# The second pass of a first batch: one order of GpSimd's work for another

## The chip, the cores and the metric

The kernel runs on one core of a Trainium2 chip. The metric is the device time of one execution in microseconds, as a median over runs of the same program. One further execution was recorded by the hardware profiler; all views of the profile are of that one.

## The reference

Two blocks follow one another. The first is an attention in which only scores close to the row's largest count; the second is a gated feed-forward layer.

```python
# q, k, v: (8, 8, 576, 64) float32; tau = 0.02
scores = scale * q @ k^T                       # scale = 1 / 8
thresh = max(scores, -1) - tau
scores = where(scores >= thresh, scores, -1e9)
attn   = exp(scores - max(scores, -1))
attn   = attn / (sum(attn, -1) + 1e-9)
x      = (attn @ v) as (4608, 512)             # heads side by side
g      = x @ w_gate                            # (512, 1536), float64 in memory
val    = x @ w_val                             # (512, 1536), float64
out    = (g * sigmoid(g) * val) @ w_out        # (1536, 512), float64
```

## The kernel before, in words

The kernel works through 8 batches of 4 pairs of heads. The first batch is special: while its attention runs, the weights come in and are turned from float64 into float32 by hand. It goes over its four pairs twice. The first pass (n = 0 to 3 in the loop over `segs[:2 * NP]`, NP = 4) does the tiles t = 0 and 1 of 128 queries of each pair; the second pass (n = 4 to 7, from about 57 to 134 us) does the tiles 2, 3 and 4, so a segment n has three steps x = 0, 1, 2. Tile 4 is half as long and holds both heads in one tile. Everything in this loop is issued in the order in which it is written, on each engine; from batch 1 on, a planner (`Plan`) with estimated durations orders the work. The planner starts after the loop and does not see its real times.

A step of the second pass makes the scores of a tile (TensorE, L465 or L471), the row maxima (VectorE, L484), the exponentials (ScalarE, L487), the mask and sums (VectorE, L492), the reciprocal `ri` of the sums (L495), and then scales p: head 0 on ScalarE (L502), head 1 on GpSimd (L500; steps 0 and 1 only, tile 4 has no second half). TensorE transposes p (L536) and, a step later, multiplies it by v (L569). Between these it fills in the first products of the feed-forward layer: four groups of `gate` (L585, "pg") and `value` ("pv"), spread over the pass by `fill`, so that one value product is finished in each segment. ScalarE copies the gate's product in two ways (L600, L601), VectorE combines them with the value's product (L609) into `hall`, and `gates` lets GpSimd multiply that by the gate (L616).

The weights go through these steps, one piece of 128 x 768 numbers at a time; 21 of 24 pieces are finished in the loop:

- `fetch_weights`: SP issues the loads into one of several places (L306, L309).
- `split_weights`: ScalarE makes a scaled upper part (L325, into the weight's place `dst`) and the lower words (L326, into `lo`, one of three places used in turn, `los`).
- `clamp_split`: GpSimd clamps the upper part (L318).
- `shift_weights`: VectorE shifts it by 3 bits (L345).
- `join_weights`: VectorE joins it with the sign (L351) and frees the place of the load; then, in the version before, GpSimd adds the lower words of one piece.
- `add_lower(n)`: GpSimd adds the lower words of n more pieces that are joined (L361). A piece that has been joined but not added is in `unsummed`.

A piece is split in one step, shifted in the next and joined in the one after. In the second pass a segment handles four pieces: at the end of step 2 of segments 4 to 6 ("double") two pieces are shifted and one more is split, so step 0 of the next segment joins two pieces, steps 1 and 2 one each. In segment 4 the scaling of the next batch's q (L398) follows step 1. The version before ends each step with `gates`, and each step begins with `join_weights`, so that GpSimd's order in a segment is: add, scale, clamp, add; add, scale, clamp; add, clamp, clamp, gate product.

After the loop what is left of the products is filled in, one more piece is joined and added, and `gates` is called once more; then the planner takes over with the last three pieces (L909 to L923) and batch 1.

Of the kernel before, what the change touches and what calls it, by code (L numbers as in the profile page):

```python
# [128 lines left out]
def kernel(  # L129
# [14 lines left out]
    NP = H // 2  # L144
# [117 lines left out]
    def give_back(ps):  # L262
        turns.append(taken.pop(id(ps))[0])

    def run_idle(n):
        ps = bank("idle")
        for _ in range(n):
            nc.tensor.matmul(ps[:, 0:TC], ones[:, 0:P], ones, start=True, stop=True)
        give_back(ps)
# [42 lines left out]
    def words(place, dst, w):  # L312
        return places[place].bitcast(U32).rearrange("p (m n w) -> p m n w", m=dst.shape[1], w=2)[:, :, :, w]

    early_slots, clamped, unclamped, shifted, unsummed = [True], [], deque(), [], []
# [16 lines left out]
    def clamp_split():  # L332
        while unclamped:
            dst = unclamped.popleft()
            clamp(nc.gpsimd, dst)
            clamped.append(dst)
# [8 lines left out]
            nc.vector.tensor_scalar(out=ub, in0=ub, scalar1=3, scalar2=None, op0=ALU.logical_shift_left)  # L345
        shifted.extend(steps)

    def join_weights():
        for up, place, lo in shifted:
            ub = up.bitcast(U32)  # L350
            nc.vector.scalar_tensor_tensor(out=ub, in0=words(place, up, 1), scalar=0x80000000, in1=ub,  # L351
                                           op0=ALU.bitwise_and, op1=ALU.bitwise_xor)
            used.discard(place)
        unsummed.extend(shifted)
        shifted.clear()
        add_lower(min(1, len(unsummed)))

    def add_lower(n):
        for up, place, lo in unsummed[:n]:
            ub = up.bitcast(U32)  # L360
            nc.gpsimd.tensor_tensor(out=ub, in0=ub, in1=lo.bitcast(U32), op=ALU.add)  # L361
            joined.append(up)
        del unsummed[:n]
# [155 lines left out]
    def flip_steps():  # L519
        if not unflipped:  # L520
            return
        seg, t, both, ps = unflipped.popleft()
        n = P if t < NT else D
        pT = pTbufs[0][:, 0:2 * KT * n].rearrange("p (h t q) -> p h t q", h=2, t=KT)
        pT2 = pTbufs[0][:, 2 * KT * n:(2 * KT + 1) * n]
        pTbufs.rotate(1)
        end = None
        for h, (p, unit) in enumerate(ps):
            tp = bank("tp")
            if h == len(ps) - 1:  # L530
                end = bank("end")
            for kt in range(KT):
                at_ = kt * P + (D if turned(t) and h == 1 else 0)
                ks, to = slice(at_, at_ + P), slice(kt * P, (kt + 1) * P)
                if unit is ident:
                    nc.tensor.transpose(tp[:, to], p[:, ks], unit)  # L536
                else:
                    nc.tensor.matmul(tp[:, to], p[:, ks], unit, start=True, stop=True)
            if t < NT:
                if h == 1 and not turned(t):  # L540
                    for hs, (p_, unit_) in zip(heads, ps):
                        nc.tensor.matmul(end[hs, 0:P], p_[:, KM:S], unit_, start=True, stop=True)
                elif h == 1:
                    nc.tensor.transpose(end[:, 0:P], both, unit)
                nc.scalar.copy(pT[:, h], tp.rearrange("p (t q) -> p t q", q=P))
            else:
                for hs in heads:
                    nc.tensor.matmul(end[hs, 0:D], p[hs, KM:S], unit[hs, hs], start=True, stop=True)
                nc.scalar.copy(pT, tp.rearrange("p (t h q) -> p h t q", h=2, q=D))
            give_back(tp)  # L550
            yield
        nc.scalar.copy(pT2, end[:, 0:n])
        give_back(end)
        unattended.append((seg, t, pT, pT2))

    def attend_tile(copy=lambda xa, fn: (fn(), give_back(xa))):
        if not unattended:
            return
        if not xts:
            for u, lo in enumerate((0, 2 * XW)):  # L560
                xts["full", u] = xall[:, lo:lo + XW].rearrange("p (c n) -> p c n", c=NCC)
            xts["last", 0] = xlast
        seg, t, pT, pT2 = unattended.popleft()
        vr, vr2 = seg["v"]
        n = pT2.shape[1]
        xa = bank("xa")
        for kt in range(KT):
            for h in range(2):
                nc.tensor.matmul(xa[h * D:(h + 1) * D, 0:n], vr[:, h, kt, :], pT[:, h, kt, :],  # L569
                                 start=(kt == 0), stop=False)  # L570
        nc.tensor.matmul(xa[:, 0:n], vr2, pT2, start=False, stop=True)
        u, lo = divmod(t * P, TC)
        to = xts[("last", 0) if t == NT else ("full", u)][:, seg["i"], lo:lo + n]
        copy(xa, lambda: nc.scalar.copy(to, xa[:, 0:n]))
# [39 lines left out]
    def gates():  # L614
        for ht, gt in ungated:
            nc.gpsimd.tensor_tensor(out=ht, in0=ht, in1=gt, op=ALU.mult)  # L616
        ungated.clear()
# [36 lines left out]
    def fill(n):  # L654
        credit[0] += n
        done = 0
        while credit[0] > 0:
            c = next(pieces)
            left[0] -= c
            done += c  # L660
            credit[0] = credit[0] - c if c else 0
            if not c:
                break
        return done
# [8 lines left out]
    def pace(n, x):  # L673

        return left[0] / (sum(len(seg["tiles"]) for seg in segs[n:2 * NP]) - x)
# [32 lines left out]
    def give(unit):  # L708
        ready.append(unit)
        left[0] += cost(unit)  # L710
# [19 lines left out]
    for n, seg in enumerate(segs[:2 * NP]):  # L730
        early_slots[0] = n < NP
        if n >= NP:
            seg["v"] = segs[seg["i"]]["v"]
        for x, t in enumerate(seg["tiles"]):
            go = scores(seg, t)
            next(go)
            if (n, x) != (NP - 2, 1):
                join_weights()
            if not n and not x:
                run_idle(6)  # L740
            next(last, None)
            box = []
            if n < NP:
                attend_tile(lambda *y: box.extend(y))
            else:
                attend_tile()
            flips = flip_steps()
            if n >= NP and x == 1:
                next(flips, None)
            next(go)  # L750
            if box:
                box[1]()
                give_back(box[0])
            next(last, None)
            for _ in flips:
                pass
            if n == NP and x == 0:
                attend_tile()
                give(FIRST)
            part = pace(n, x) / 2  # L760
            more = len(split)
            if n or x:
                split_weights()
                fetch_weights(2)
            next(go)
            if (n, x) == (NP - 2, 1):
                join_weights()
            if (n, x) == (NP - 2, 0):
                prepare(segs[n + 1])
            clamp_split()  # L770
            add_lower(1)
            double = t == NT and NP <= n < NP + 3
            if more and not double:
                shift_weights()
            fill(part)
            next(go)
            fill(part)
            if double:
                shift_weights(2)
                split_weights()  # L780
                clamp_split()
                fetch_weights(2)
            gates()
            last = go
            if n == NP - 1 and x == 0:
                later.rotate(1)
            if later and (n == NP or n == NP - 1 and x == 0):
                to, fr = later.popleft()
                nc.vector.transpose(out=to, in_=fr)
            if x == 0 and 0 < n < NP - 1:  # L790
                load_v(segs[n + 1])
                more_loads.popleft()()
            if n == 0 and x == 1 or n == 1:
                scales.popleft()()
            elif n == NP - 2 and x == 1:
                more_loads.popleft()()
                scales.popleft()()
            elif n == NP - 1:
                scales.popleft()()
                fetch_qk(NP)  # L800
            elif n == NP and x == 1:
                scales.popleft()()
            if x == len(seg["tiles"]) - 2 and n + 1 < len(segs) and (n, x) != (NP - 2, 0):
                prepare(segs[n + 1])
# [1391 lines left out]
```

## Time and profile before

| What | Value |
|---|---|
| runs | 1370.12 us median of three (1370.07, 1370.12, 1372.92) |
| profiled execution | 1367.33 us, its span 1365.5 us |
| granted TensorE clock | 0.999 of full speed |
| busy: TensorE, VectorE, ScalarE, GpSimd | 99%, 79%, 63%, 52% of the span |
| TensorE busy, 56.9 to 79.8 us | 21.75 of 22.9 |
| TensorE busy, 79.8 to 99.4 us | 18.58 of 19.6 |
| TensorE busy, 99.4 to 119.0 us | 18.13 of 19.6 |
| GpSimd busy in the same three stretches | 16.62, 16.74, 16.70 |

Each line of the page's groups and of a timeline gives the line of the code, the engine, the operation, the tile written and the tile read, and a duration. A timeline adds the start, and in square brackets the idle time of the engine ahead of the instruction with what ended it. A row of the stretches gives the stretch, its length, the busy time of TensorE, of its weight loads, of VectorE, ScalarE and GpSimd with the number of instructions, the granted clock, the share of the DMA engines and GB/s. In the chain that ended last, each row is a start, a time and what the program's end depended on in that time.

### The profile page before, as it was taken

Reading aid. Unit: us, or ns where it says so; the run is one execution under the profiler, and the core shown is the slowest. Engines: PE = TensorE matmul, PEld = TensorE weight load, DVE = VectorE, ACT = ScalarE, POOL = GpSimd, SP = SyncE. Lnnn points to the kernel's source line nnn. Section 1 sums busy time; section 2 is a strip of 40 time slices with the busy share of each in tenths; the row PEclk is TensorE's granted clock in tenths of the full one; section 3 lists DMA queues with packets and bytes.
Section 4 is the critical chain, followed back from the end, with each engine's and each line's share of the span. In section 5 each row is a group of like instructions: output and inputs, shape, how many; then the busy total and the mean of one; then the engine's idle time right before and its main releaser. Section 6 shows DMA issues by size and latency. Waiting matters only on the chain.

```text
span 1365.5 us, 39125 instructions
## 1 busy us (share of the span) xinstructions
PE 1347.5 (99%) x15590; PEld 1124.9 (82%) x15590; DVE 1076.7 (79%) x2860; ACT 866.7 (63%) x2222; POOL 715.7 (52%) x664
## 2 busy tenths in 40 slices
PE   8999999999999999999999999999999999999998
PEld 6777787777788788878888788888887788999888
DVE  7878998888787877787878877887788766797786
ACT  6888765677765777677767676677767673330330
POOL 2788698754655669434963387337943592000000
PEclk9999999999999999999999999999999999999999
DMA  8752424556425441654155514542255404424411
GB/s 175 202 186 88 85 49 125 142 164 179 111 52 162 146 90 36 193 144 113 38 170 135 161 19 144 149 145 66 78 155 146 109 27 160 149 75 143 159 54 32
DMA packets 208293, 162.31 MB, mean 119 GB/s; under 512 B 166128, under 2 KB 180464, under 8 KB 202736
## 3 DMA queue, kind: packets, MB, share of 16 engines
q1 hardware_dynamic: 203920, 158.86, 40.9%
q8 instruction: 123, 2.02, 0.6%
q10 hardware_dynamic: 4192, 0.95, 0.3%
q14 instruction: 58, 0.48, 0.1%
HBM read 138.28 MB, written 21.50 MB: 117 GB/s over the span
## 4 chain that ended last, share of the span: by engine, by line
PE 90%; DVE 3%; POOL 2%; DMA 2%; ACT 1%; issue 1%; SPq 1%; ACTq 0%; DVEq 0%; POOLq 0%
PE pb L1031 17%; PE pa L1031 12%; PE px L1520 12%; PE sc L1780 10%; PE pe L1031 9%; PE xa L1917 9%; PE po L1313 5%; PE py L1529 5%; PE pg L1244 2%; PE pv L1244 2%; PE sc L1198 1%; PE pe L1198 1%; PE sc L1031 1%; PE sc L465 1%; POOL pall L500 1%
## 5 line engine op out<-in xcount | busy, mean ns | idle before, releaser
L1861 DVE SCALAR_TENSOR_TENSOR pall<-sc,th,pall 128x288 f32<-128x288 f32 x504 | 244.2, 513 | 49.1 <-ACT pall L1859 32.5
L1859 ACT ACTIVATE pall<-sc,lows 128x288 f32<-128x288 f32 x504 | 233.8, 500 | 72.9 <-DVE pall L1861 38.0
L1031 PE MATMUL pb<-xall,big 128*128 128x256 f32 x1104 | 262.0, 380 | 0.0
L1031 PEld LDWEIGHTS pb<-xall,big 128*128 128x128 f32 x1104 | 207.5, 190 | 29.6 <-issue 1.6
L1896 DVE STREAM_TRANSPOSE pall<-pall 128x576 f32<-128x576 f32 x252 | 188.0, 763 | 27.7 <-POOL pall L1891 14.3
L1894 ACT ACTIVATE pall<-pall,ri 128x288 f32<-128x288 f32 x416 | 190.6, 526 | 23.4 <-DVE ri L1882 22.5
L1031 PE MATMUL pa<-xall,big 128*128 128x256 f32 x752 | 178.9, 381 | 0.3 <-ACT sc L1038 0.3
L1031 PEld LDWEIGHTS pa<-xall,big 128*128 128x128 f32 x752 | 140.7, 190 | 20.9 <-issue 2.5
L882 POOL TENSOR_TENSOR hall<-hall,tmp 128x512 f32<-128x512 f32 x80 | 102.5, 1281 | 103.1 <-DVE hall L1090 60.3
L1780 PE MATMUL sc<-kT,qT 64*32 64x288 f32 (+1 forms) x5376 | 145.7, 345 | 0.1
L1818 DVE TENSOR_REDUCE mx<-sc 128x2 f32<-128x576 f32 x168 | 118.4, 746 | 34.7 <-PE sc L1780 34.1
L1891 POOL TENSOR_SCALAR pall<-pall,ri 128x288 f32<-128x288 f32 x88 | 87.8, 1006 | 103.9 <-DVE ri L1882 74.7
L1780 PEld LDWEIGHTS sc<-kT,qT 64*32 64x32 f32 x5376 | 98.2, 106 | 50.2 <-issue 11.2
L1031 PE MATMUL pe<-xall,big 128*128 128x256 f32 x576 | 138.4, 383 | 0.5 <-ACT pall L1894 0.5
L1917 PE MATMUL xa<-pall,vall 64*32 64x288 f32 x4032 | 129.4, 404 | 3.0 <-PE px L1520 2.7
L1031 PEld LDWEIGHTS pe<-xall,big 128*128 128x128 f32 x576 | 107.6, 190 | 19.3 <-issue 4.3
L1917 PEld LDWEIGHTS xa<-pall,vall 64*32 64x32 f32 x4032 | 83.4, 107 | 41.7 <-issue 5.0
L882 POOL TENSOR_TENSOR tmp<-tmp 128x512 f32<-128x512 f32 x36 | 45.9, 1274 | 85.8 <-ACT tmp L1112 85.8
L1876 ACT COPY sums<-sums 32x6 f32<-32x6 f32 x336 | 66.6, 198 | 28.3 <-DVE pall L1861 24.2
L1089 ACT ACTIVATE vall<-tmp 128x512 f32<-128x512 f32 x96 | 60.0, 628 | 35.3 <-DVE tmp L1102 28.1
L1529 PE MATMUL py<-wo,hall 128*128 128x256 f32 x336 | 74.8, 379 | 0.0
L882 POOL TENSOR_TENSOR hall<-hall 128x384 f32<-128x384 f32 (+2 forms) x67 | 67.4, 1020 | 9.0 <-PE px L1520 8.2
(273 smaller groups left out, 2492.4 us busy)
## 6 DMA issues: line engine op xcount, KB each, us to landing
big<-sums_hbm SPq DMA_DIRECT2D x42, 1024.0 KB, 5.2
big<-sums_hbm SPq DMA_DIRECT2D x48, 768.0 KB, 4.6
vall<-in_v_dram SPq DMA_DIRECT2D x112, 144.0 KB, 3.1
out_dram<-big SPq DMA_DIRECT2D x32, 256.0 KB, 3.1
qT<-in_q_dram SPq DMA_DIRECT2D x112, 72.0 KB, 4.8
kT<-in_k_dram SPq DMA_DIRECT2D x112, 72.0 KB, 3.0
wo<-in_moe_w_gate_dram SPq DMA_DIRECT2D x16, 384.0 KB, 3.9
wo<-in_moe_w_val_dram SPq DMA_DIRECT2D x16, 384.0 KB, 4.8
```

Of the source, the lines that this page charges most:

```text
L882: return lambda: nc.gpsimd.tensor_tensor(out=out, in0=a, in1=b, op=op)
L1031: nc.tensor.matmul(ps[:, i], w[:, k_, i * P:(i + 1) * P], x[:, k_, :], start=first and i == k_ == 0, stop=True, skip_group_check=True)
L1520: nc.tensor.matmul(ps, a[:, f, :], ws[n][:, f, :], start=bank_ not in begun, stop=True, skip_group_check=True)
L1529: nc.tensor.matmul(ps(), a[:, f, i * P:(i + 1) * P], operands[o][:, f, :], start=first and f == 0, stop=True, skip_group_check=True)
L1780: nc.tensor.matmul(to[g * G:(g + 1) * G], qT[hs, col:col + G], kT[hs, c * SH + lo:c * SH + hi], start=True, stop=True)
L1818: rs.append(job("DVE", 0.72 if w > 1 else 0.42, lambda h=h: nc.vector.tensor_reduce(out=mx[:, n0 + h:n1 + h + 1:max(2, n1 - n0), 0], in_=s ...
L1859: ej = job("ACT", 0.44, lambda x=x, n=n: nc.scalar.activation(ps[x], scs[x], AF.Exp, bias=nm[:, n:n + 1]), ej, rank=top, on=on[x])
L1861: masks[x] = job("DVE", 0.48, lambda x=x, n=n: nc.vector.scalar_tensor_tensor(out=ps[x], in0=scs[x], scalar=th[:, n:n + 1], in1=ps[x], op0 ...
L1891: scaled.append(job("POOL", 1.02, lambda x=x, n=n: nc.gpsimd.tensor_scalar(out=x, in0=x, scalar1=ri[:, n:n + 1], scalar2=None, op0=ALU.mul ...
L1894: scaled.append(job("ACT", 0.46, lambda x=x, n=n: nc.scalar.activation(x, x, AF.Copy, scale=ri[:, n:n + 1]), rj, rank=rank))
L1896: seg["turned"].append(job("DVE", 0.72, lambda both=both: nc.vector.transpose(out=both, in_=both), *scaled, rank=rank))
L1917: nc.tensor.matmul(holds[a].ap()[x * G:(x + 1) * G, 0:SH].rearrange("d (i q) -> d i q", q=G), vr[rs, h, j, ds], p[rs, h, :, j, :], start=( ...
```

## The change

In the second pass only, GpSimd's instructions of a step change their order. `join_weights` adds no lower words there; after the scale of p and the clamp, up to two pieces are added, and then the gate products that are waiting are multiplied, instead of at the end of the step. A value product that is finished in a step is therefore multiplied by its gate in the next one. GpSimd's order in a segment becomes: scale, clamp, add, add, gate product; scale, clamp, add; clamp, add, clamp. The first pass and everything behind the loop are as before.

```diff
-    def join_weights():
+    def join_weights(add=1):
...
-        add_lower(min(1, len(unsummed)))
+        add_lower(min(add, len(unsummed)))
...
             if (n, x) != (NP - 2, 1):
-                join_weights()
+                join_weights(n < NP)
...
             clamp_split()
-            add_lower(1)
+            add_lower(1 if n < NP else 2)
+            if n >= NP:
+                gates()
             double = t == NT and NP <= n < NP + 3
             if more and not double:
                 shift_weights()
...
                 split_weights()
                 clamp_split()
                 fetch_weights(2)
-            gates()
             last = go
```

## The prediction, made before the changed kernel was run

> **What bounds the kernel now.** I read the page first. TensorE is busy for 1347.5 us of the span of 1365.5, so a change off TensorE counts only where it makes TensorE wait.
>
> ```profile
> PE 1347.5 (99%) x15590; PEld 1124.9 (82%) x15590; DVE 1076.7 (79%) x2860; ACT 866.7 (63%) x2222; POOL 715.7 (52%) x664
> ```
>
> Next I looked up the engines by stretch. The changed pass runs from about 57 to 134 us; one of its segments (n = 6) and the stage behind it:
>
> ```profile
> 99.40:119.00 19.60, 18.13 (x140) 13.87 (x139) 16.23 (x31) 17.20 (x33) 16.70 (x12) 1.00 0.16 47
> 152.00:400.00 248.00, 247.13 (x3276) 197.62 (x3284) 209.94 (x598) 171.96 (x480) 169.98 (x166) 1.00 0.42 114
> ```
>
> In the segment TensorE idles 1.47 us of 19.6, and GpSimd (the fifth busy time, 16.70) is nearly full. Behind the pass TensorE idles 0.87 us of 248. So what the pass loses, nothing later gives back. Third, the chain that ended last, through segment 6 (start, us, what):
>
> ```profile
> 99.36 1.87 POOL pall L500
> 101.23 1.32 POOL big L318
> 102.55 2.63 POOL big L361 x2
> ...
> 106.10 2.03 POOL pall L500
> ...
> 108.17 0.66 PE tp L536 x4
> ...
> 108.94 2.17 PE pv L585 x10
> ...
> 111.14 0.69 DVE hall L609
> 111.82 0.64 DVE wo L345 x2
> ...
> 112.68 1.41 DVE lows L484 x2
> 114.09 2.83 DVE wo L351 x2
> 116.92 0.75 DVE pall L492 x2
> ```
>
> This cycle of 19.6 us bounds the pass: from step 0's scale of p (L500) over GpSimd's clamp and two adds to step 1's scale, transposes and products, then VectorE's shifts (L345), maxima, joins (L351) and masks, to the next segment's scale. Fourth, the timelines of GpSimd and VectorE, for the order and the long instructions:
>
> ```profile
> 84.73 1.83 POOL L361 TENSOR_TENSOR big<-big 128x768 uint32<-128x768 uint32 x1
> 89.33 1.83 POOL L361 TENSOR_TENSOR big<-big 128x768 uint32<-128x768 uint32 x1
> 91.20 0.83 POOL L318 TENSOR_SCALAR big<-big 128x768 f32<-128x768 f32 x1
> 94.37 1.27 POOL L616 TENSOR_TENSOR hall<-hall,tmp 128x512 f32<-128x512 f32 x1
> 96.53 2.46 POOL L361 TENSOR_TENSOR big<-big,extra 128x768 uint32<-128x768 uint32 x1 [0.89 <-DVE big L351]
> ```
>
> ```profile
> 75.80 1.96 DVE L351 SCALAR_TENSOR_TENSOR big<-wo,big 128x768 uint32<-128x768 uint32 x2
> 85.47 1.51 DVE L345 TENSOR_SCALAR big<-big 128x768 uint32<-128x768 uint32 x1
> 87.57 0.94 DVE L351 SCALAR_TENSOR_TENSOR big<-wo,big 128x768 uint32<-128x768 uint32 x1
> 92.19 1.02 DVE L345 TENSOR_SCALAR big<-big 128x768 uint32<-128x768 uint32 x2
> 94.46 2.86 DVE L351 SCALAR_TENSOR_TENSOR big<-wo,big 128x768 uint32<-128x768 uint32 x2
> ```
>
> The reader is to see that shift and join shut out GpSimd's add and gate product, and the other way round. A shift takes 0.51 (1.02 for two); the one of 85.47 took 1.51 because the add of 84.73 ran until 86.56. Two joins take 1.96; those of 94.46 took 2.86 because the gate product ran until 95.64. The add of 96.53 took 2.46 for 1.83 because the second join ran until 97.3. An engine that waits gets in when the other's instruction ends, ahead of that one's next.
>
> **The change part by part.** T is the start of step 0's scale, U that of step 1's.
>
> *First add moved behind the scale.* In segments 5 to 7 the start of T is not GpSimd's: the reciprocal (L495) ends at 79.63, 99.19 and 118.79, and the scale starts 0.17 after it each time (the chain names a matmul there; the constant gap says otherwise). So moving the add gives T nothing directly.
>
> *Gate product moved out of the joins.* It no longer stands at the end of step 2, where it held up the joins of segments 6 and 7 (2.86 and 2.04 + 0.95 against 1.96). Gain 0.9 us each in segments 6 and 7; none in segment 5, whose joins took 1.96 already.
>
> *Between the two scales.* Before: scale 1.87, clamp 1.3, step 0's second add and step 1's first add, 3.6; together 6.73 (79.81 to 86.54, and again 99.36 to 106.10). After: scale, clamp, two adds (both of step 0), then the waiting gate product, 1.27. A shift waits there already (T + 5.66, during the second add); it gets in ahead of the gate product with 0.44 (86.54 to 86.98). So U = T + 8.4: 1.7 us more. This is on the path: step 1's reciprocal ends at 85.56, so its scale already waits 0.8 us for GpSimd, and the transposes wait for the scale. Charged in segments 5, 6, 7; in segment 4 no gate product is pending yet and its second scale (66.06) follows its reciprocal, so nothing.
>
> *Step 2's add moved behind the clamp, step 1's behind its scale.* After U's scale (2.03) GpSimd now has clamp 0.82, add 1.82, clamp 0.82, and starts the add at U + 5.5. Before, both adds were done by 91.16 and the port was free when the two shifts came at 92.19, which is U + 5.65. Now the first shift meets an add that runs until U + 7.3: 1.7 us, on the path. Segments 5 and 6. In segment 4 the same happens by another way: before, add 70.62 to 72.45, clamp until 73.56, second shift at 73.59. After, step 1's add (1.82) goes ahead of the scaling of q (1.72), step 2's clamp ends at about 73.4, the add follows until 75.2, and the second shift, which waits for the clamp's signal, comes after it: 1.6 us. In segment 7 the two shifts at the end don't exist; its shift of step 2 (1.29) is held by an add either way.
>
> *ScalarE's splits.* The ring of lower words has three places. In step 0 of segments 5 to 7 the split now stands in the program ahead of the add that reads that place, so its wait (L326 behind the add: 1.2, 1.6, 1.6 us) goes. The add then takes the newer piece's words, which changes the lowest bits and no duration. That wait was not on the path, so I take no gain. In its place step 1's split waits for step 0's second add, until T + 6.8 (before: no wait), and ScalarE's scale of p, the copies of the gate's products and step 2's exponentials are queued behind it. It ends near T + 8.6; the transposes need it with U's scale only, which ends past T + 10.3: cover 1.7 us, cost zero. If that cover were gone, the excess would be paid in full.
>
> *Loads.* SP's fetches of weights stand where they stood, behind joins, and slide with them. That matters at the end: the last fetch (133.24) waits for the last join (132.18 to 133.16), and the next q and k loads stand behind it, so the delay is handed on. GpSimd's work at the very end has a gap of 1.66 us ahead of L923 as cover for the reordered add and gate product: zero, 0 to 1.
>
> Sum: segment 4, +1.6; segment 5, 1.7 + 1.7 = +3.4; segment 6, 1.7 + 1.7 - 0.9 = +2.5; segment 7, 1.7 - 0.9 = +0.8. Total +8.3. The profiled execution took 1367.33 us (span 1365.5 and 1.8 around it) and would take 1375.6; the three runs lie at 1370.07 to 1372.92, so on their median 1370.12 I forecast 1378.4.
>
> Two costs are unknown. (a) At the end of step 2 a clamp waits for the port with the two shifts; no row shows whether a waiting GpSimd instruction gets in between two of VectorE's. If it does, 0.82 more in each of segments 4 to 6; never less than zero, since the clamp is needed later than the shifts. I take zero, since step 2's second pieces come late from ScalarE (93.58 before). (b) Step 2's join now waits during the gate product and starts with U's scale. A scaling by a per-partition value (L398 at 42.73) took 1.78 where its like takes 1.08, under a join (41.19 to 43.55): +0.7. But U's scale at 86.54 stood 0.44 under a shift and took 2.03 for 1.87: +0.16. I take zero, the nearer row being the second, with up to 0.5 more in segments 5, 6 and 7.
>
> The Trainium skill, page "SBUF — State Buffer", section "Who interferes with whom", has VectorE and GpSimd share one port pair that whoever issues first keeps for the whole instruction, the other being fully blocked. The adds agree, but the scale of p does not: the join of 87.57 ran its usual 0.94 inside the scale of 86.54 to 88.57. By the page's rule the scale would lose a whole join of 0.87 in (b), and the sum would be about +10.9.
>
> **The rivals.**
> *VectorE first.* The margin in step 2 is 0.16 us (U + 5.65 against U + 5.5). If the shifts ask for the port just before the add starts, and both pass, the 1.6 and twice 1.7 go: +3.3, 1373.4. For it: the margin is small. Against: three segments have to fall so. If some do: +5 to +6.6.
> *Harder waits.* (a) and (b) in full: 8.3 + 3 x 0.82 + 3 x 0.5 = +12.3, 1382.4. For it: waiting engines do get in at a hand-over.
> *Not slower: the joins' gain alone.* If GpSimd's longer queue in step 0 is hidden, what is left is -0.9 in segments 6 and 7: 1368.3, within 0.2%. It decides at step 1's reciprocal, T + 5.75: the scale would have to find GpSimd free by then. Even at their shortest (clamp 0.82) the instructions ahead of it need 1.87 + 0.82 + 3.64 + 1.27 = 7.6, so it needs the gate product to be elsewhere. Against it stands that the value product of each segment ends in step 2 (L609 at 91.59), so its gate product is always pending at the next step 0.
> *The change does nothing*: the order is written out, and no planner can undo it; I give this no chance of its own.
>
> **How the numbers follow.** Forecast 0.50 (1376 to 1380); harder waits 0.20; VectorE first, in all or some segments, 0.20; the joins' gain alone 0.06; unpriced gain 0.04. A measurement can tell about 0.2%, 2.7 us. Slower: 0.50 + 0.20 + 0.13 (those of VectorE first that stay above 2.7) = 0.83. Same: 0.07 + 0.06 = 0.13. Faster: 0.04. The range goes from VectorE first less the runs' scatter, 1372, to the harder waits, 1383.
>
> **What would show it.** In the profile after: T to U 8.4 us (6.7 before), with two adds and the gate product in it; the joins of step 0 at 1.96 in each segment; step 2's first shift (or the pair) long by 1.7, over an add; the wait of L326 gone in step 0 and there in step 1; a segment near 22 us; TensorE idle some 8 us more before 145 us and the same after. I am wrong if the pair of shifts is still at 1.02, if T comes early enough to pay for the gate product, or if TensorE's idle time behind the pass shrinks.

## The result, and the profile after

The changed kernel takes 1377.32 us (median of six, 1376.99 to 1378.31) against 1370.17 for the kernel before: a ratio of 1.0052, 95% interval 1.0041 to 1.0064, or 7.15 us slower. A second set of runs of the same kernel gave 1378.59 against 1370.61, ratio 1.0065 (1.0052 to 1.0078). The forecast was +8.3 us (1378.4). The profiled executions lie 9.66 us apart (1376.99 and 1367.33).

The page's first line and two of the stretches, segment 6 with its surroundings and the 248 us behind the pass:

```profile
PE 1352.2 (98%) x15590; PEld 1130.0 (82%) x15590; DVE 1079.2 (78%) x2860; ACT 867.8 (63%) x2222; POOL 715.2 (52%) x664
```

```profile
100.00:122.00 22.00, 18.77 (x129) 14.27 (x130) 14.43 (x29) 15.69 (x29) 16.68 (x11) 0.84 0.13 42
160.00:408.00 248.00, 247.50 (x3269) 198.01 (x3272) 210.24 (x600) 172.30 (x480) 170.01 (x166) 1.00 0.41 114
```

Behind the pass TensorE idles 0.50 us of 248 (0.87 before): the loss is made in the pass and kept. But TensorE is busy 4.7 us longer than before with the same 15590 products, and the granted clock in the segment is 0.84. That is new, and the forecast does not have it. The chain through segment 6:

```profile
101.91 1.87 POOL pall L500
103.78 1.31 POOL big L318
105.09 2.63 POOL big L361 x2
...
108.61 1.60 POOL hall L616
110.21 2.41 POOL pall L500
...
112.67 1.12 PE tp L536 x4
...
114.00 4.27 PE pv L585 x10
```

The gate product (L616) stands between the two scales, as forecast. The products behind the second transposes took 4.27 us where they took 2.17. VectorE's long instructions, and GpSimd's around step 2 of segment 5:

```profile
72.48 2.16 DVE L345 TENSOR_SCALAR big<-big 128x768 uint32<-128x768 uint32 x1 [0.72 <-POOL big L318]
93.74 3.06 DVE L345 TENSOR_SCALAR big<-big 128x768 uint32<-128x768 uint32 x2
98.06 1.81 DVE L351 SCALAR_TENSOR_TENSOR big<-wo,big 128x768 uint32<-128x768 uint32 x2
118.91 1.02 DVE L345 TENSOR_SCALAR wo<-wo 128x768 uint32<-128x768 uint32 x2
```

```profile
93.46 1.82 POOL L361 TENSOR_TENSOR big<-big 128x768 uint32<-128x768 uint32 x1
95.32 1.07 POOL L318 TENSOR_SCALAR big<-big 128x768 f32<-128x768 f32 x1
108.61 1.60 POOL L616 TENSOR_TENSOR hall<-hall,tmp 128x512 f32<-128x512 f32 x1
110.19 2.42 POOL L500 TENSOR_SCALAR pall<-pall,ri 128x576 f32<-128x576 f32 x1
```

The shift of segment 4 waits for the add (2.16 for 0.56), the pair of segment 5 takes 3.06 for 1.02, and the joins are down to 1.81. In segment 6 the pair is at 1.02, unhindered. TensorE's timeline says why:

```profile
78.88 2.09 PE L465 MATMUL sc<-pall 64*128 64x288 f32 x10 [2.21 <-DVE pall L492]
112.67 1.12 PE L536 MATMUL tp<-pall 128*128 128x128 f32 x4 [1.60 <-POOL pall L500]
113.79 4.47 PE L585 MATMUL pv<-xall,big 128*128 128x256 f32 x10
136.09 3.77 PE L585 MATMUL pv<-xall,big 128*128 128x256 f32 x10
```

After idle time of 2.21 us, and of 0.97 and 1.60 and of 0.72 and 0.88 a little apart, TensorE ran at a granted clock of 0.50 for a while: at 81 to 84.5, 111 to 119 and 135 to 139 us by stretches of 1 us. Products that are late by 2 us bring the shifts past the add.

The table compares intervals, read from the timelines: S is segment 4's second scale, T and U the scales of steps 0 and 1 of a segment, J the last join of the pass. A star marks an interval in which the clock stood at 0.50 for part of the time.

| | S to T5 | T5 to U5 | U5 to T6 | T6 to U6 | U6 to T7 | T7 to U7 | U7 to J | S to J |
|---|---|---|---|---|---|---|---|---|
| before | 13.75 | 6.73 | 12.82 | 6.74 | 12.86 | 6.73 | 6.49 | 66.12 |
| after | 15.17 | 7.97* | 13.80 | 8.29 | 14.84* | 8.45 | 7.02* | 75.54 |
| after, second profile | 15.17 | 7.98* | 13.81 | 8.29 | 14.20 | 8.35* | 5.35 | 73.15 |
| gate product alone | 13.59 | 8.29 | 12.18 | 8.46 | 12.18 | 8.31 | 5.34 | 68.35 |
| the same, second profile | 13.59 | 8.28 | 14.45* | 8.28 | 13.94* | 8.30 | 5.35 | 72.19 |
| adds alone | 15.32 | 8.11* | 14.72 | 7.19* | 14.52 | 8.11* | 6.71 | 74.68 |
| no add in step 2 | 13.58 | 8.29 | 12.16 | 8.46 | 12.18 | 8.29 | 5.35 | 68.31 |

J is VectorE's end of the pass, not TensorE's. TensorE's first product of the next batch (`pg`) starts 2.90 us behind J before the change (135.08) and 3.72 or 3.73 behind it in all the other rows of the table. So the delay that TensorE carries on is 0.8 us more than S to J shows.

### The profile page after: what moved, and what is told of

It is laid out like the page before. It is cut to its first block, busy times and chain, and to the rows that moved or that the text cites. A ratio compares the mean times of both kernels' runs of the same rounds, so it can differ in the third digit from the quotient of the medians.

```text
span 1374.9 us, 39125 instructions
## 1 busy us (share of the span) xinstructions
PE 1352.2 (98%) x15590; PEld 1130.0 (82%) x15590; DVE 1079.2 (78%) x2860; ACT 867.8 (63%) x2222; POOL 715.2 (52%) x664
## 3 DMA queue, kind: packets, MB, share of 16 engines
q8 instruction: 123, 2.02, 0.6%
## 4 chain that ended last, share of the span: by engine, by line
PE 90%; DVE 2%; POOL 2%; DMA 2%; issue 1%; SPq 1%; ACT 1%; ACTq 0%; DVEq 0%; POOLq 0%
PE pb L1032 17%; PE pa L1032 12%; PE px L1521 12%; PE sc L1781 10%; PE pe L1032 9%; PE xa L1918 9%; PE po L1314 5%; PE py L1530 5%; PE pg L1245 2%; PE pv L1245 2%; PE sc L1199 1%; DMA vall<-in_v_dram 1%; PE pe L1199 1%; PE sc L1032 1%; PE pv L585 1%
```

## The experiments

Two theories stood against each other. The queue theory is that of the prediction: GpSimd's order and the port that it shares with VectorE make the loss. The clock theory says that most of it is TensorE at half clock, which the longer waits set off. Each median stands against the kernel before on the same chip (1369.73 for the first four, 1370.61 for the next four).

**The two halves of the change.** First the gate product alone:

```diff
             add_lower(1)
+            if n >= NP:
+                gates()
...
-            gates()
+            if n < NP:
+                gates()
```

> Only the gate product moves, to behind the adds of the next step; the adds stay where they were. Queue theory (GpSimd's longer queue and the port it shares with VectorE set the time): between the scales of steps 0 and 1 +1.3 to +1.7 us in segments 5, 6 and 7, the joins of segments 6 and 7 short again (-0.9 each), nothing in step 2: +2 to +3.3 us in all. Clock theory (the granted TensorE clock falling to 0.50 after idle time makes most of the loss): the idle time ahead of the second transposes grows here as in the whole change, so the clock falls and the cost is 4 us or more, with a mean granted clock below 0.998.

Median 1375.77, ratio 1.0053 (1.0037 to 1.0068), so +6.0; but the six executions scatter from 1371.83 to 1379.47. The profile is of the fastest: the clock is at 1.00 throughout and S to J is 2.23 longer, as the queue theory has it (1.6 between the scales, 0.6 to 1.2 back behind each). So the median spoke for the clock and the profile for the queue. A second profile was to show whether both are true:

> The kernel with the gate product alone moved, a second profile: the first had the clock at 1.00 throughout and lost 2.2 us between segment 4's second scale and the last join, while its executions scatter by 7.6 us. If falls of the clock make that scatter, this look shows one or more stretches at half clock in the pass or none, and the same 8.3 us between the scales in every segment without one; each stretch adds 0.6 to 1.7 us.

It took 1375.37, beside 1368.66 for the kernel before, and has two stretches at half clock in the intervals of the table (a third, from 43.6 to 47.0, lies ahead of them). The second transposes of segment 5 and the products behind them, in the first profile and then in the second:

```profile
90.44 0.66 PE L536 MATMUL tp<-pall 128*128 128x128 f32 x4 [2.62 <-POOL pall L500]
...
91.05 2.32 PE L585 MATMUL pv<-xall,big 128*128 128x256 f32 x10
```

```profile
91.50 1.12 PE L536 MATMUL tp<-pall 128*128 128x128 f32 x4 [2.61 <-POOL pall L500]
...
92.62 3.40 PE L585 MATMUL pv<-xall,big 128*128 128x256 f32 x10
```

The same idle time of 2.6 us ahead of the same products is followed by the full clock in one execution and by half of it in the other. U5 to T6 is 12.18 and 14.45, U6 to T7 12.18 and 13.94: the two stretches cost 2.3 and 1.8 us, and S to J is 6.07 longer than before instead of 2.23. Each cost more than the 0.6 to 1.7 that was expected. Why the same pause costs this once and not the other time is told in the last section.

Then the adds alone:

```diff
-                join_weights()
+                join_weights(n < NP)
...
-            add_lower(1)
+            add_lower(1 if n < NP else 2)
```

> Only the adds move, behind scale and clamp; the gate product stays at the end of a step. Queue theory: the two scales stay 6.7 us apart; step 2's shifts wait for an add (+1.6 in segment 4, +1.7 each in segments 5 and 6), and the joins of segments 6 and 7 come after the gate product (-0.9 each): +3 us in all, with rows of L345 near 3 us. Clock theory: no more idle time ahead of the second transposes than before, the clock stays at 1.00, and the cost is 0 to +1.6.

Median 1378.78, ratio 1.0071 (1.0055 to 1.0087): +9.0, more than the whole change. Both expectations are missed. The clock falls in segments 5, 6 and 7, at about the start of their first scales. Apart from that the queue costs more than was thought:

```profile
97.01 2.70 DVE L345 TENSOR_SCALAR big<-big 128x768 uint32<-128x768 uint32 x2
...
100.96 2.35 DVE L351 SCALAR_TENSOR_TENSOR big<-wo,big 128x768 uint32<-128x768 uint32 x2
```

The pair of shifts waits for the add and the joins still wait for the gate product, which ran from 100.36 to 101.63. So the two waits add up where the gate product stays, and moving it saves the second.

> The kernel with the adds alone moved, a second profile: the first lost 8.6 us in the pass with three stretches at half clock. Queue theory: in segments without such a stretch the scales are 6.7 us apart and the next segment begins 13.6 to 14.5 us later (12.8 before). Clock theory: the clock falls again in every segment where the loss is, and a segment without a fall takes 19.6 us, as before.

1378.55; the same picture, S to J 74.58, with a fall of the clock in each of segments 5 to 7, as the clock theory expected. T6 to U6 is 6.73 in spite of a stretch at half clock in it, and U5 to T6 and U6 to T7 are 15.35 and 14.67 without one: the clock falls in the first part of these segments and the loss is in the second as well. But 15.35 and 14.67 are above the 13.6 to 14.5 of the queue theory too. Products that are late in the first part of a segment may hold up its second part, so these intervals alone don't decide between the two.

**Step 2's add left out.**

```diff
-            nc.vector.scalar_tensor_tensor(out=ub, ..., scalar=0x80000000, in1=ub, op0=ALU.bitwise_and, op1=ALU.bitwise_xor)
+            nc.vector.scalar_tensor_tensor(out=ub, ..., scalar=0 if drop else 0x80000000, in1=ub,
+                                           op0=ALU.bitwise_and, op1=ALU.bitwise_and if drop else ALU.bitwise_xor)
...
+        if drop:                    # step 2 of segments 4 to 6
+            joined.extend(...)      # no add
+            shifted.clear()
```

> The changed kernel without step 2's add in segments 4 to 6 (the join writes zeros into these three pieces of weights, which leaves them out of the products). Queue theory: the shifts of step 2 find the port free: -1.6 in segment 4, -2.0 in segment 5, nothing in segment 6, where the add was done before the shifts; +3.5 to +4 us over the kernel before. Clock theory: the idle time ahead of the second transposes stays, and so do 6 us or more of the loss.

Median 1373.89, ratio 1.0032 (1.0021 to 1.0044): +4.2, a little above the queue theory's +3.5 to +4 and far from the 6 or more of the clock theory. The profile has no stretch at half clock, though the idle time ahead of the second transposes is as in the whole change (0.97 and 1.60 in segment 5), and the pair of shifts is unhindered:

```profile
95.08 1.02 DVE L345 TENSOR_SCALAR big<-big 128x768 uint32<-128x768 uint32 x2
```

S to T5 is back at 13.58, and with it the stretch at half clock at the start of segment 5 is gone: it came from the add of segment 4, which kept TensorE waiting for 2.21 us at 76.67.

**Three of the four gate products left out.**

```diff
-            if n >= NP:
-                gates()
+            if n > NP:
+                ungated.clear()
```

> The changed kernel without three of its four gate products in this pass (the value products stay unmultiplied there, so part of the first groups of the result is left out). Queue theory: the scales of steps 0 and 1 are 6.7 to 7.1 us apart again in segments 5 to 7, 1.2 to 1.6 us less each; the add ahead of step 2's shifts stays, so +3 to +5 us over the kernel before remain. Clock theory: with less idle time ahead of the second transposes the clock stays at 1.00 in the profile and +2 us or less remain.

Median 1377.92, ratio 1.0057 (1.0042 to 1.0072): +7.3, above both expectations. T6 to U6, the one such interval without a slow stretch, is 6.74, so the gate product is the whole of what was added there. But S to T5 is 15.17 as in the whole change, and the clock falls in segments 5 and 7 for 6.8 us each. In this profile, the slowest of the six executions (1380.91), the clock took what the queue gave back. That doesn't explain the median: the two executions with the highest mean granted clock (0.997 and 0.998) took 1377.52 and 1378.31, the fastest (1374.62) had 0.995. Why so much of the loss stays without the gate products is open.

**TensorE kept running.**

```diff
+            for _ in range(warm[h]):
+                nc.tensor.matmul(tp[:, 0:TC], ones[:, 0:P], ones, start=True, stop=True)
...
-            flips = flip_steps()
+            flips = flip_steps((3, 6) if n > NP and x == 2 else (0, 0))     # later (2, 2)
```

> The changed kernel with idle products (three and six of 128 x 256) ahead of the two transposes of step 2 in segments 5 to 7, so that TensorE has work while it waits there. Clock theory: the granted clock stays near 1.00 there and the loss falls below +2.5 us. Queue theory: the stretch at half clock behind the second scale of segment 6 cost 2.7 us but spared 1.7 of port wait, that of segment 7 cost 0.8; without them +5 to +5.5 us.

> The changed kernel with two idle products ahead of each of the two transposes of step 2 in segments 5 to 7 (0.9 us each, less than the idle time of 1.0 and 1.6 there; three and six were too many). Clock theory: no stretch at half clock behind the second scale, and the loss falls to +4 us or less. Queue theory: without the slow stretch segment 6 gets its products back sooner and its shifts meet the add again (L345 near 3 us, as in segment 5), so the loss stays at +6 to +8 us.

Medians 1387.02 and 1383.63, ratios 1.012 (1.0101 to 1.0138) and 1.0105 (1.0088 to 1.0122): both slower by far, and neither theory expected that. With three and six the clock did stay at 1.00 in the pass, but the idle products were no cover:

```profile
90.82 2.86 PE L533 MATMUL tp<-pall 128*128 128x256 f32 x12 [0.22 <-ACT tmp L603]
```

Six of them are twelve in the profile and take 2.86 us, and they start only when ScalarE has emptied their bank, so they hold the transposes up. With two and two, the clock fell all the same, at about the start of segments 5 and 7. As a test of the clock this is inconclusive.

**The changed kernel again.**

> The changed kernel itself once more, beside the others and with a second profile. Queue theory: the intervals of the pass (8.0 to 8.5 us between the scales, 1.7 to 2.1 us of port wait at the shifts of segments 4 and 5) come back as they were, and the median is +6 to +9 us; where the clock falls may differ, and where it does not fall in segment 6 the shifts there are held by the add instead. Clock theory: the loss follows the length of the stretches at half clock; without them it is under +3 us.

Median +8.0. The intervals come back to 0.02 us up to U6, as the queue theory had it. In segment 6 the clock does not fall this time, and there the port wait comes in its place:

```profile
118.02 3.06 DVE L345 TENSOR_SCALAR wo<-wo 128x768 uint32<-128x768 uint32 x2
```

U6 to T7 is 14.20 with the port wait and 14.84 with the slow stretch.

**The gate product on VectorE.** The idle time of VectorE in step 2 was left over by every version:

```diff
+            if n > NP and x == 2:
+                gates(nc.vector)      # behind join_weights()
...
-            gates()                   # at the end of each step
```

> The kernel before, with the gate products of the pass multiplied by VectorE behind step 2's join of the next segment, where VectorE waits 0.7 us for ScalarE, instead of by GpSimd at the end of step 2. Queue theory: the joins of segments 6 and 7 take 1.9 instead of 2.9, and nothing else grows by more than 0.5: 0.5 to 1.2 us faster than the kernel before, perhaps too little to tell. Clock theory: the same time as before, since the clock stood at 1.00 there already.

Median 1368.38, ratio 0.9987 (0.9978 to 0.9996): 2.2 us below the other median, and about 1.8 by the ratio, a little more than was expected.

```profile
86.78 0.68 DVE L616 TENSOR_TENSOR hall<-hall,tmp 128x512 f32<-128x512 f32 x1
...
90.53 1.07 DVE L345 TENSOR_SCALAR big<-big 128x768 uint32<-128x768 uint32 x2
92.86 1.81 DVE L351 SCALAR_TENSOR_TENSOR big<-wo,big 128x768 uint32<-128x768 uint32 x2
```

The product takes 0.68 us in a gap, the joins 1.81, and S to J is 64.49, 1.63 less than before. By the ratio's interval this version is a little faster than the kernel before, and so faster than the changed one. In its profile TensorE then idles 2.8 us near 150 us, behind a load of weights that landed at 145.2, and the clock falls there too.

## Why the prediction was right

The time, its sign and most terms held; where the sum came from was right by its own steps, with one mechanism missing.

*Segment 4, +1.6:* S to T5 grew by 1.42, and the second shift took 2.16, over the add, as written.

*Between the scales, +1.7 each:* without a slow stretch the interval is 8.29 (segment 6), +1.55. The shift got in ahead of the gate product there, which shows in the product's 1.60 us. In segment 5 the exponentials came late from a slow TensorE, the gate product went first, and the interval was 7.97.

*Step 2's add, +1.7:* right in segment 5, with 2.04 instead (3.06 less 1.02). The difference is due to unknown (a), which is settled: a waiting clamp does get in between two of VectorE's instructions (95.32, between the two shifts). In segment 6 the first profile shows the pair at 1.02, which the prediction had named as a sign of being wrong; the second profile has 3.06 there, so this was the slow products' doing. Unknown (b) is real too: U's scale took 2.42 for 2.02 in segment 6, 0.4 of the 0.5 allowed.

*The joins, -0.9:* they took 1.81 against 2.86, a gain of 1.05.

*ScalarE and the loads:* the wait of L326 left step 0 and came to step 1 (0.91 and 1.09 us); the second transposes still waited for GpSimd, so the cover held. The last fetch started at 141.55, behind the last join (140.50 to 141.48), and the delay was handed on.

*Segment 7, +0.8:* T7 to U7 grew by 1.72, as written, but the prediction put nothing behind it, and U7 to J shrank to 5.35 where the clock did not fall (-1.14). I take it, from the order of the rows, that VectorE's shift and two transposes of that step were done while the second scale waited; the same 5.34 or 5.35 stands in three of the experiments' profiles. TensorE got back only 0.3 of the 1.14, since its first product of the next batch follows J by 0.8 more.

Without slow stretches the intervals add up to 1.42 + 1.56 + 0.98 + 1.55 + 1.34 + 1.72 - 1.14 = +7.4 us, with T5 to U5 taken as 8.29 from the experiment without step 2's add, U6 to T7 and U7 to J from the second profile. With the 0.8 behind J it is 8.2 us for TensorE; the forecast was 8.3.

*What was missing* is the step "TensorE idle some 8 us more". Of 9.4 us that the span grew, 4.7 are busy time, at half clock; in the second profile 2.3 of 9.3. In the two profiles of the whole change the stretches moved S to J to +9.42 and +7.03, that is by +2.0 and -0.4 from the 7.4: small, because late products spare port waits and let the gate product pass. In the gate product's experiment, with less to spare, two of them cost 3.8 us. So in the first profile the sum came out right partly because port and clock stand in for one another.

The executions without a profile have their mean granted clock on record, and a stretch of 3.41 us at half clock takes 0.00125 off it (1.71 us lost of some 1370). The changed kernel took 1378.59 in an execution at 0.999, so with one such stretch at most, 1377.49 and 1377.94 at 0.998, and 1378.31 and 1379.97 at 0.992 and 0.993; the six between took 1376.80 to 1379.05. So its loss is there almost without the clock, and hardly follows it. With the gate product alone the time does follow the clock: 1371.83 at 1.000, 1374.54 to 1375.92 at 0.997, 1379.09 and 1379.47 at 0.995.

*The rivals:* VectorE first did not happen in segments 4 and 5, and where the shifts of segment 6 were free it was by slow products. Harder waits happened in part. The joins' gain alone is what the last experiment got, by taking the product off GpSimd.

## What to carry to other kernels

When an instruction moves in a full queue, price each place that it comes to by what shares its port there, not by its own duration: here 1.3 us of product and a moved add became 7 us. A wait that lengthens TensorE's pauses (here to more than 1 us within 3.4 us) can have a second price, the clock, and whether it is paid hangs on where the pause falls, so compare several profiles, and the mean clock of every execution, before a loss is put down to one cause. Work for which a queue has no room may fit into another engine's wait, even at the same port.

## What the runs showed of the hardware

Every stretch at half clock in and around the pass is 3.41 us long or twice that (1.71 or 3.41 us of lost clock, by stretches of 1 us). Within one profile the stretches also begin whole multiples of 3.41 us apart: 80.98, 111.70 and 135.59 us in the first profile of the change are 9 and 7 times 3.41 apart. So time can be cut into windows of 3.41 us on this grid, and the idle time of TensorE counted in each. The pause of 2.6 us in segment 5 of the gate product's experiment lies within one window in the second profile (2.49 us idle from 87.97 to 91.39, then half clock); in the first, a window's end at 89.05 cuts it (1.23 us idle in the window ahead, 1.39 in the one behind), and the clock stays. Over the pass in all profiles, each of the eight windows at full clock with 1.93 us idle or more was followed by half clock, and none with 1.04 or less; between these, nine were and others, up to 1.72, were not. The rest of the rule is open. The Trainium skill, page "TensorE: Matmul & The Clock Gate", section "What's actually happening", has the clock halved after an idle window of about 3.4 us that runs freely; the length and the free running agree, but windows that were idle for less than their whole length, 1.05 to 2.49 us, were enough here.

On the shared port, the waiting engine gets in at the next boundary on either side: a shift between an add and a product (the product, asked for at 108.61, took 1.60 us for 1.27), a clamp between two shifts (95.32, in the pair of 3.06).
